# Moving half of the first layer's operand sums to GpSimd, and first-layer pieces two by two between the products

## The chip, the cores and the metric

The kernel runs on one core of a Trainium2 chip. The metric is the device time of one execution in microseconds (us), as the median of several runs. Engines are named as in the profile: PE is TensorE's matmuls and PEld its weight loads, DVE is VectorE, ACT is ScalarE, POOL is GpSimd, and SP is SyncE, which only issues DMAs here.

## What is computed

A small attention between tokens and states feeds a mixture of eight experts whose routing weights P come from a Sinkhorn iteration. Cut to what matters:

```python
# attention: x is (8, 8, 512, 64), state is (8, 8, 32, 64); their outputs side by side are 4352 rows of 512
logits = x @ w_gate                     # (N, 8), N = 4352
P = np.exp(logits - logits.max())
for _ in range(8):                      # Sinkhorn: rows, then columns
    P /= P.sum(1, keepdims=True) + 1e-09
    P /= P.sum(0, keepdims=True) + 1e-09
    P *= N / E
for e in range(8):
    h = np.maximum(x @ w1[e], 0.0)      # (N, 1024)
    ye = h @ w2[e]                      # (N, 512)
    out += P[:, e:e + 1] * ye
```

Every expert sees every row. The rows come in nine blocks: eight of 512 token rows, and one of 256 state rows.

## The kernel before

Up to about 142 us the kernel runs attention, routing and expert 0 in an order that a planner (`issue`, with costs and due times written into each `op`) lays out before launch. None of that part is touched. It ends with the first layer of (expert 1, block 0) and with Pmat, the routing weights.

Behind it lies the main part: `work` is a list of 63 units (experts 1 to 7, nine blocks each), and the order of each engine's instructions is the order in which the loop at the end of the kernel emits them. Each engine takes its instructions strictly in that order. Unit i runs the second layer of `work[i]` and, woven into it, the first layer of `work[i+1]` and the projection of `work[i+2]`.

**The second layer** (`layer2`) multiplies a 512 x 1024 hidden block by a 1024 x 512 matrix. It uses seven half-size products in place of eight (a Winograd scheme): the block and the matrix are cut in two by two, sums of the parts are multiplied, and the products are put together. In order, the seven products write the PSUM tiles A, E, Bseed, A, Bseed, E, Bseed (matmuls of line 271; PSUM is the accumulator memory that matmuls write). Each is eight matmuls of 256 columns, or four in block 8. After the first, ScalarE copies A into one of two Bseed tiles (line 305), on which later products pile up. After each of the other six, VectorE adds P times the product to `acc` in SBUF, one or two instructions of line 285 (in0 in PSUM, in1 in SBUF). A product that writes a tile again waits for the adds that read it.

**The operand sums.** The hidden tile is `Hm[128, 2, 4, 512]`: two halves of the hidden features (index i), four chunks of 128 (index j), and the tokens. The scheme needs sums of its quarters, s1, s2 and s4 in the tile `sm`, and a21 in place in `Hm`:

```python
nc.vector.tensor_add(s1, a21, a22)      # line 244
nc.vector.tensor_sub(a21, a11, a21)     # line 245
nc.vector.tensor_sub(s2, s1, a11)       # line 246
nc.vector.tensor_sub(s4, a12, s2)       # line 247
```

They are made in two halves of four instructions, for j = 0, 1 and for j = 2, 3, each 512 columns wide in float16 (256 for block 8). E, the second product, reads s1; the third (Bseed) reads s2; the fifth reads a21 and the sixth reads s4. Each of these takes its j = 0, 1 weights first.

**The first layer** (`layer1`) is a generator of eight pieces. A piece (0 to 7: j = 0 with i = 0, 1, then j = 1, and so on) makes 128 hidden features of a block: two matmuls of 512 columns (line 219), and a ReLU on ScalarE from PSUM to `Hm` (line 238). Its PSUM tiles come from a ring of four banks that the projection shares. The first half of the sums is emitted behind the fourth piece, and the second half behind the eighth. How many pieces follow each product stands in the loop as `(0, 0, 1, 2, 2, 2, 1)`; behind each `step()` a step of the weight loader can come.

**The projection** (`project`, lines 204 and 208) makes V, which the first layer of a token block reads: 16 narrow matmuls, put behind the first product, and four casts on ScalarE. Block 8 needs none, so the units of block 6 and the last two units have no projection.

**GpSimd** has three jobs in this part. `weigh` (line 254) multiplies the rows of `acc` by expert 0's weight, four instructions for each block (two for block 8), emitted in the units of expert 1: blocks 0 and 1 in the first unit, then block bi + 1 in unit bi. `load_w` issues the DMAs of the next expert's weights (lines 166 and 168) from block 1 on. They go through GpSimd's queue. And ten steps of the loop's count after that, with a step every sixth `step()`, VectorE makes the eight differences T of the second weight matrix (line 178); those left at the end of block 6 are emitted at once.

Of the kernel before, what the change touches and what calls it, by code (L numbers as in the profile page):

```python
# [12 lines left out]
ALU = mybir.AluOpType  # L13
AF = mybir.ActivationFunctionType
EPS = 1e-9


class Ring:
# [71 lines left out]
def kernel(  # L90
# [9 lines left out]
    nc = tc.nc  # L100
# [32 lines left out]
    def bank(shape, dtype, name, tag="bank"):  # L133
        return pools[tag].tile(shape, dtype, name=name, tag=tag)
# [25 lines left out]
    def load_w(e):  # L160

        w1h = mw.tile([128, NKC, F], FP16, name="w1h", tag="w1h")
        w2h = mw.tile([128, NFB, Dm], FP16, name="w2h", tag="w2h")
        w16[e] = (w1h, w2h)
        for g in range(2):
            nc.gpsimd.dma_start(out=w1h[:, ds(2 * g, 2), :], in_=w1r[e, :, ds(2 * g, 2), :])  # L166
        for g in range(2):
            nc.gpsimd.dma_start(out=w2h[:, ds(NJ * g, NJ), :], in_=w2r[e, :, ds(NJ * g, NJ), :])
        for _ in range(10):
            yield  # L170
        T = tpool[0].tile([128, 4, NJ, DH], FP16, name="T", tag="T")
        tsum[e] = T
        b11, b12 = w2h[:, :NJ, :DH], w2h[:, :NJ, DH:]
        b21, b22 = w2h[:, NJ:, :DH], w2h[:, NJ:, DH:]
        for i, (p, q) in enumerate(((b12, b11), (b22, T[:, 0]), (b22, b12), (b21, T[:, 1]))):
            for g in range(2):
                jj = ds(g * (NJ // 2), NJ // 2)
                nc.vector.tensor_sub(T[:, i, jj], p[:, jj], q[:, jj])
                yield
# [12 lines left out]
    def project(e, bi):  # L192
        if bi == B:
            return
        w1h = w16[e][0]
        V = vpool.tile([128, NQ, F], FP16, name="V", tag="V")
        vt[(e, bi)] = V
        for f in range(F // 512):
            cols = ds(f * 512, 512)
            ps = [bank([128, 512], FP32, "v_ps", ring[0]) for _ in range(NQ)]  # L200
            for j in range(4):
                for q in range(NQ):
                    r = ((j ^ q) % 2) * 64
                    nc.tensor.matmul(ps[q][ds(j * Ns, Ns), :], stT[ds(r, 64), bi, q, ds((j ^ q) * Ns, Ns)],  # L204
                                     w1h[ds(r, 64), 2 * q + j // 2, cols],
                                     tile_position=(r, j * Ns))
            for q in range(NQ):
                nc.scalar.copy(out=V[:, q, cols], in_=ps[q])  # L208

    def hidden_ps(e, bi, fb, out):  # L210
        w1h = w16[e][0]
        cols = ds(fb * 128, 128)
        if bi < B:
            V = vt[(e, bi)]
            terms = [(V[:, q, cols], aT[:, bi, q]) for q in range(NQ)]
        else:
            terms = [(w1h[:, kc, cols], xsT[:, kc]) for kc in range(NKC)]
        for k, (lhs, rhs) in enumerate(terms):
            nc.tensor.matmul(out, lhs, rhs, start=(k == 0), stop=(k == len(terms) - 1))  # L219
# [6 lines left out]
    def layer1(e, bi):  # L226

        t0, tn = blocks[bi]
        th = tn // 2
        Hm = hpool.tile([128, 2, NJ, S], FP16, name="Hm", tag="Hm")  # L230
        sm = hpool.tile([128, 3, NJ, S // 2], FP16, name="sm", tag="sm")
        hid[(e, bi)] = (Hm, sm)
        for j in range(NJ):
            for i in range(2):
                fb = i * NJ + j
                hps = bank([128, S], FP32, "hps", "h")
                hidden_ps(e, bi, fb, hps[:, :tn])
                nc.scalar.activation(out=Hm[:, i, j, :tn], in_=hps[:, :tn], func=AF.Relu)  # L238
                if j % 2 and i:
                    jj = ds(j - 1, 2)  # L240
                    a11, a21 = Hm[:, 0, jj, :th], Hm[:, 0, jj, th:tn]
                    a12, a22 = Hm[:, 1, jj, :th], Hm[:, 1, jj, th:tn]
                    s1, s2, s4 = (sm[:, k, jj, :th] for k in range(3))
                    nc.vector.tensor_add(s1, a21, a22)  # L244
                    nc.vector.tensor_sub(a21, a11, a21)  # L245
                    nc.vector.tensor_sub(s2, s1, a11)  # L246
                    nc.vector.tensor_sub(s4, a12, s2)  # L247
                yield

    def weigh(b):  # L250
# [92 lines left out]
    def op(rank, on, emit, after=(), takes=(), uses=(), also=()):  # L343
        o = Op(rank, on, emit, after, takes, uses, also)
        ops.append(o)
        return o
# [126 lines left out]
    for b in range(B):  # L473
# [23 lines left out]
        for q in range(NQ):  # L497
# [71 lines left out]
            s1 = op(r(4), {"DVE": (0.60, 0.80)}, subA, [m1], [], [eA, mxA])  # L569
# [71 lines left out]
    def tile_of(tag, shape):  # L641
        sm_[tag] = gsb.tile(shape, FP32, name=tag, tag=tag)
        return sm_[tag]
# [14 lines left out]
    for it in range(8):  # L658
        def rownorm():
            rsum = tile_of("rsum", [128, NTB])  # L660
            nc.vector.reduce_sum(out=rsum, in_=Pmat, axis=AX_X)
            nc.vector.tensor_scalar(out=rsum, in0=rsum, scalar1=EPS, scalar2=None, op0=ALU.add)
            nc.vector.reciprocal(out=rsum, in_=rsum)
# [5 lines left out]
        def colnorm(csb=csb):  # L669
            crec = tile_of("crec", [128, E])  # L670
            nc.vector.tensor_scalar(out=crec, in0=csb.tile, scalar1=EPS, scalar2=None, op0=ALU.add)
            nc.vector.reciprocal(out=crec, in_=crec)
# [176 lines left out]
    def step():  # L849
        nonlocal n  # L850
        n += 1
        if n % 6 == 0 and wload:
            try:
                next(wload[0])
            except StopIteration:
                wload.pop(0)

    work = [(e, bi) for e in range(1, E) for bi in range(len(blocks))]
    for i, (e, bi) in enumerate(work):
        if bi == 1 and e + 1 < E:  # L860
            wload.append(load_w(e + 1))
        l2 = layer2(e, bi, i)
        l1 = layer1(*work[i + 1]) if i + 1 < len(work) and work[i + 1] not in hid else iter(())
        for k in range(7):
            next(l2)
            step()
            if k == 0 and i + 2 < len(work) and work[i + 2] not in vt:
                project(*work[i + 2])
            for _ in range((0, 0, 1, 2, 2, 2, 1)[k]):
                next(l1, None)  # L870
                step()
        for part in (l1, l2):
            for _ in part:
                pass
        if bi == len(blocks) - 3:
            for _ in (x for w in wload for x in w):
                pass
            wload.clear()
# [30 lines left out]
```

## Time and profile before

| | |
|---|---|
| Time, three runs | 768.05 us median (767.78 to 769.49) |
| The profiled execution: time / span from first to last instruction | 766.84 us / 764.9 us |
| Granted TensorE clock over the span | 1.000 |
| Busy in an ordinary unit of 10.23 us (409.13 to 419.36) | PE 10.23, PEld 7.11, DVE 8.39, ACT 7.00, POOL 0.23 |
| Busy from 144 to 196 us (units of expert 1) | PE 52.00, PEld 35.52, DVE 45.09, ACT 35.47, POOL 51.99 |

A page of the profile lists each engine's busy time, then the span in 40 slices, the DMA queues, the chain of work that ended last, and groups of instructions. A row of a group reads: line, engine, operation, output<-inputs, shape, count | busy us in all, mean ns of one | idle us of the engine just before them, and who ended that idle time. A row of the chain reads: start, length, and what the chain went through. A row of a timeline reads: start, length, engine, line, operation. Matmul ends are modelled and overlap the next start, so the length of a product is best taken from start to start.

### The profile page before, as it was taken

The page shows a single profiled execution, that of the slowest core. Times are in us where ns is not written, and L with a number is a line of the kernel's source. Part 1 is how long each engine was busy: PE and PEld are TensorE (multiplying, and loading weights), DVE is VectorE, ACT ScalarE, POOL GpSimd, SP SyncE. Part 2 cuts the span into 40 slices and gives each one's busy share as a digit, 9 for nine tenths or more (in the row PEclk, how much of TensorE's full clock was granted, in tenths as well). Part 3 has the DMA queues.
Part 4 walks back from the last instruction along what each step waited for, and adds up shares of the span by engine and source line. Part 5 has one row for each costly group of instructions (what it writes and reads, how often), then busy time and mean ns, then how long its engine had stood idle before and what let it go on. Part 6 is the DMA issues. An engine that isn't in the chain of part 4 may idle for free.

```text
span 764.9 us, 16309 instructions
## 1 busy us (share of the span) xinstructions
PE 747.9 (98%) x6561; PEld 501.8 (66%) x6561; DVE 629.9 (82%) x1544; ACT 513.7 (67%) x1003; POOL 104.6 (14%) x102
## 2 busy tenths in 40 slices
PE   5999999999999999999999999999999999999997
PEld 3444445566776667766776767766677667766775
DVE  5998977888987888888887888888887888878886
ACT  5878976666667675766657666676657676576662
POOL 4433100799200000100001000100001000000000
PEclk9999999999999999999999999999999999999999
DMA  8997200060015000510006000240006000012234
GB/s 136 184 152 120 49 1 1 1 112 1 1 25 88 1 2 1 91 21 2 1 1 111 2 1 1 44 69 1 2 1 108 4 2 1 1 55 86 85 108 138
DMA packets 41595, 34.61 MB, mean 45 GB/s; under 512 B 16688, under 2 KB 33072, under 8 KB 41520
## 3 DMA queue, kind: packets, MB, share of 16 engines
q0 software_dynamic: 21248, 20.97, 17.7%
q1 hardware_dynamic: 19040, 12.08, 6.4%
q8 instruction: 51, 0.84, 0.4%
q10 hardware_dynamic: 1232, 0.52, 0.3%
q14 instruction: 24, 0.20, 0.1%
HBM read 42.48 MB, written 8.91 MB: 67 GB/s over the span
## 4 chain that ended last, share of the span: by engine, by line
PE 90%; DVE 5%; ACT 3%; DMA 1%; issue 0%; POOL 0%; POOLq 0%
PE hps L219 27%; PE Bseed L271 20%; PE E L271 14%; PE A L271 13%; PE yps L756 7%; PE v_ps L204 4%; PE hps L721 4%; DVE acc L285 2%; DMA x_nat<-in_x_dram 1%; DVE sm L244 1%; ACT V L357 1%; ACT Hm L238 1%; PE su_ps L596 1%; PE v_ps L699 0%; ACT xT L357 0%; PE ET_ps L581 0%
## 5 line engine op out<-in xcount | busy, mean ns | idle before, releaser
L238 ACT ACTIVATE Hm<-hps 128x512 f16<-128x512 f32 (+1 forms) x496 | 266.0, 572 | 188.5 <-PE hps L219 173.4
L219 PE MATMUL hps<-aT,V 128*128 128x512 f16 x880 | 234.8, 379 | 0.0
L271 PEld LDWEIGHTS <-Hm 128*128 128x128 f16 x1904 | 186.2, 98 | 69.8 <-issue 0.8
L285 DVE SCALAR_TENSOR_TENSOR acc<-Bseed,Pmat,acc 128x256 f32<-128x256 f32 x357 | 156.9, 479 | 56.9 <-PE Bseed L271 54.4
L271 PEld LDWEIGHTS <-sm 128*128 128x128 f16 x1428 | 134.2, 98 | 52.5 <-DVE sm L244 24.2
L271 PE MATMUL Bseed<-T,Hm 128*128 128x256 f16 x952 | 124.5, 273 | 0.4 <-DVE acc L285 0.3
L271 PE MATMUL A<-w2h,Hm 128*128 128x256 f16 x952 | 124.7, 273 | 0.0
L219 PEld LDWEIGHTS <-V 128*128 128x128 f16 x880 | 86.1, 98 | 45.2
L208 ACT CAST V<-v_ps 128x512 f16<-128x512 f32 x216 | 111.3, 610 | 0.0
L285 DVE SCALAR_TENSOR_TENSOR acc<-E,Pmat,acc 128x256 f32<-128x256 f32 x238 | 104.3, 477 | 3.7
L244 DVE TENSOR_TENSOR sm<-Hm 128x512 f16<-128x512 f16 (+1 forms) x124 | 51.7, 417 | 19.1 <-ACT Hm L238 18.3
L756 PE MATMUL yps<-w2h,hT 128*128 128x512 f16 x272 | 66.5, 380 | 0.0
L285 DVE SCALAR_TENSOR_TENSOR acc<-A,Pmat,acc 128x256 f32<-128x256 f32 x119 | 52.4, 479 | 15.8 <-PE A L271 15.7
L271 PE MATMUL E<-T,sm 128*128 128x256 f16 x476 | 64.5, 274 | 0.7
L271 PE MATMUL Bseed<-T,sm 128*128 128x256 f16 x476 | 62.4, 273 | 0.0
L271 PE MATMUL E<-w2h,sm 128*128 128x256 f16 x476 | 62.3, 273 | 0.0
L254 POOL TENSOR_SCALAR acc<-acc,Pmat 128x512 f32<-128x512 f32 x34 | 55.2, 1638 | 44.8 <-DVE Pmat L673 44.8
L166 POOL DMA_DIRECT2D w1h<-in_moe_w_dram x12 | 8.6, 721 | 355.2 <-PE hps L219 355.2
L247 DVE TENSOR_TENSOR sm<-Hm,sm 128x512 f16<-128x512 f16 (+1 forms) x124 | 53.1, 428 | 4.2
L245 DVE TENSOR_TENSOR Hm<-Hm 128x512 f16<-128x512 f16 (+1 forms) x124 | 51.6, 416 | 4.3
L246 DVE TENSOR_TENSOR sm<-sm,Hm 128x512 f16<-128x512 f16 (+1 forms) x124 | 50.0, 403 | 0.0
L305 ACT COPY Bseed<-A 128x512 f32<-128x512 f32 (+1 forms) x63 | 34.4, 546 | 18.8 <-PE A L271 17.3
(107 smaller groups left out, 554.1 us busy)
## 6 DMA issues: line engine op xcount, KB each, us to landing
w1h<-in_moe_w_dram POOLq DMA_DIRECT2D x16, 512.0 KB, 7.2
w2h<-in_moe_w_dram POOLq DMA_DIRECT2D x16, 512.0 KB, 7.5
out_dram<-acc SPq DMA_DIRECT2D x32, 256.0 KB, 2.8
x_nat<-in_x_dram POOLq DMA_DIRECT2D x16, 256.0 KB, 6.3
st_st<-in_state_dram SPq DMA_DIRECT2D x1, 256.0 KB, 4.2
st_st<-in_state_dram ACTq DMA_DIRECT2D x1, 256.0 KB, 4.6
out_dram<-acc SPq DMA_DIRECT2D x4, 64.0 KB, 1.9
out_dram<-acc ACTq DMA_DIRECT2D x4, 64.0 KB, 2.1
```

Source lines behind the costliest of these rows:

```text
L208: nc.scalar.copy(out=V[:, q, cols], in_=ps[q])
L219: nc.tensor.matmul(out, lhs, rhs, start=(k == 0), stop=(k == len(terms) - 1))
L238: nc.scalar.activation(out=Hm[:, i, j, :tn], in_=hps[:, :tn], func=AF.Relu)
L244: nc.vector.tensor_add(s1, a21, a22)
L245: nc.vector.tensor_sub(a21, a11, a21)
L246: nc.vector.tensor_sub(s2, s1, a11)
L247: nc.vector.tensor_sub(s4, a12, s2)
L254: nc.gpsimd.tensor_scalar(out=acc[:, k, :], in0=acc[:, k, :], scalar1=Pmat[:, k, 0:1], scalar2=None, op0=ALU.mult)
L271: nc.tensor.matmul(dst[:, c], lhs(j, c), rhs[:, j], start=first and c == 0 and j == 0, stop=(j == NJ - 1), skip_group_check=True)
L285: nc.vector.scalar_tensor_tensor(out=dst, in0=src[:, c], scalar=p[:, k], in1=dst, op0=ALU.mult, op1=ALU.add)
L305: nc.scalar.copy(out=Bb[:, :nk], in_=A[:, :nk])
L756: nc.tensor.matmul(yps.tile, hT[fb].tile[:, ds(tk * 128, 128)], w2h[:, fb, :], start=(fb == 0), stop=(fb == NFB - 1))
```

## The change

The four sums of the first half (j = 1) are issued on GpSimd and not on VectorE; those of the second half (j = 3) stay on VectorE. This holds for the 62 first layers that the loop makes, and not for the one in the planner's part. The pattern of pieces changes from one, two, two, two and one behind products 3 to 7 to two behind each of products 3 to 6, and none behind the seventh. So the second half of the sums stands in VectorE's queue ahead of the seventh product's adds, where it stood behind them.

```diff
+PAT = (0, 0, 2, 2, 2, 2, 0)
...
-                    nc.vector.tensor_add(s1, a21, a22)
-                    nc.vector.tensor_sub(a21, a11, a21)
-                    nc.vector.tensor_sub(s2, s1, a11)
-                    nc.vector.tensor_sub(s4, a12, s2)
+                    (nc.vector if j > 1 else nc.gpsimd).tensor_add(s1, a21, a22)
+                    (nc.vector if j > 1 else nc.gpsimd).tensor_sub(a21, a11, a21)
+                    (nc.vector if j > 1 else nc.gpsimd).tensor_sub(s2, s1, a11)
+                    (nc.vector if j > 1 else nc.gpsimd).tensor_sub(s4, a12, s2)
...
-            for _ in range((0, 0, 1, 2, 2, 2, 1)[k]):
+            for _ in range(PAT[k]):
```

All lines behind the new one stand one number higher in the changed kernel: its sums are lines 245 to 248. In the built program GpSimd's queue runs, behind the planner's part: 8 weighings, 4 sums, 4 weighings, 4 weight DMAs, 4 sums, 4 weighings, 4 sums, and so on by fours to 2 weighings and 4 sums; then four sums for each unit, with four DMAs once for each expert. ScalarE's and SyncE's orders are the same as before.

## The prediction

> **What bounds the kernel now.** I read the page first: its busy shares and the chain that ended last.
>
> ```profile
> PE 747.9 (98%) x6561; PEld 501.8 (66%) x6561; DVE 629.9 (82%) x1544; ACT 513.7 (67%) x1003; POOL 104.6 (14%) x102
> ...
> PE 90%; DVE 5%; ACT 3%; DMA 1%; issue 0%; POOL 0%; POOLq 0%
> ```
>
> TensorE is never idle for long and GpSimd nearly always. So I next read the chain in order of time, for two stretches behind 144 us, where the 63 units (7 experts x 9 blocks) run:
>
> ```profile
> 194.49 0.87 PE A L271 x8
> 195.36 0.56 PE v_ps L204 x16
> 195.92 1.01 PE E L271 x8
> 196.93 0.87 PE Bseed L271 x8
> 197.80 0.43 PE hps L219 x2
> ...
> 203.62 0.34 DVE T L178
> 203.96 1.57 DVE acc L285 x4
> 205.53 0.34 DVE sm L244
> 205.87 0.05 issue
> 205.91 0.83 PE E L271 x6
> ```
>
> A product takes 0.87 us, a first-layer piece 0.43, a projection 0.56; the chain passes from one to the next without a gap. By matmul starts an ordinary unit is 10.23 us (409.13 to 419.36). The only loss is where E waits for the second-half sums: in the second stretch, a unit without a projection (block 6), E takes 1.12 us from its first matmul to the next product's. There are eight such units, each losing 0.22 to 0.25, and all products together lose some 2.7 us behind 144 us. That is all that relief of VectorE can bring: 0.35%.
>
> **What moves.** 62 first layers have two halves of four sums each. The first half, 248 operations, leaves VectorE, where one of 512 columns takes 0.42 (103 us in all), for GpSimd. The groups by shape price it:
>
> ```profile
> L244 DVE TENSOR_TENSOR sm<-Hm 128x512 f16<-128x512 f16 x110 | 47.6, 433 | 19.1 <-ACT Hm L238 18.3
> L254 POOL TENSOR_SCALAR acc<-acc,Pmat 128x512 f32<-128x512 f32 x34 | 55.2, 1638 | 44.8 <-DVE Pmat L673 44.8
> L559 POOL TENSOR_TENSOR a<-eA,rA 128x512 f16<-128x512 f32 x12 | 12.5, 1045 | 52.6 <-DVE rA L556 20.9 <-DVE nsB L535 12.9 <-ACT V L357 5.8
> L539 DVE TENSOR_TENSOR eA<-eA,mxA 128x512 f32<-128x512 f32 x16 | 11.4, 710 | 0.1
> ```
>
> No GpSimd operation with two float16 inputs is in the trace. Nearest is L559: two inputs, 512 columns, 1.045. Farther off are the weighing (one input, 1.64) and a 128-column memset (0.20, so 0.8 for four). I take 1.045; the ends are 0.8 and 1.64. The built program makes the second and fourth sum wait for the one before on GpSimd; a wait costs about 0.1 (Pmat ends at 138.00, the weighing starts at 138.11). Four sums: 4 x 1.045 + 0.2 = 4.4 us. The Trainium skill (GPSIMD Engine Reference, section 3.1) gives 4497 ns for an add of 2048 float32 columns, a quarter of which is 1.12, an estimate; the sum below would be 4 us larger by it.
>
> **The two engines get in each other's way.** The timeline shows it twice:
>
> ```profile
> 84.14 1.04 POOL L559 TENSOR_TENSOR a<-eA,rA 128x512 f16<-128x512 f32 x1 [12.90 <-DVE nsB L535]
> ...
> 84.61 1.13 DVE L539 TENSOR_TENSOR eA<-eA,mxA 128x512 f32<-128x512 f32 x1
> ```
>
> ```profile
> 150.69 0.88 DVE L244 TENSOR_TENSOR sm<-Hm 128x512 f16<-128x512 f16 x1 [0.18 <-ACT Hm L238]
> 151.61 0.43 DVE L245 TENSOR_TENSOR Hm<-Hm 128x512 f16<-128x512 f16 x1
> ```
>
> L539 needs 0.69 alone; started inside a GpSimd operation it ended 0.54 after that one's end, so it got its data only then. A float16 sum should end some 0.28 after the GpSimd operation it meets. Under the weighing a sum takes 0.42 or up to 0.98, and a weighing that a sum got into 1.93 to 2.00 in place of 1.55. L285, with one operand in PSUM, stays at 0.47: the adds are free of it. The Trainium skill (SBUF — State Buffer, "Who interferes with whom") says that a VectorE instruction with two SBUF inputs and a GpSimd one that reads SBUF exclude each other, whole instructions. The two-input pair agrees; the weighing does not, since sums of 0.42 run wholly inside one. By the rule alone, sums in (a) would wait out weighings of up to 1.55; the trace excludes it, so it has no chance of its own.
>
> **An ordinary unit, in us from its first A.** New order: A 0, projection 0.97, E 1.53, Bseed 2.41, two pieces 3.28, A 4.15, two pieces 5.02, Bseed 5.88, two 6.75, E 7.62, two 8.49, Bseed 9.36, end 10.23. A ReLU starts 0.65 after its piece, lasts 0.60, the second of a pair starts 0.49 later: the fourth ends at 6.76, the eighth at 10.23. GpSimd: s1 to 7.9, a21 to 9.05, s2 to 10.1, s4 to 11.25. VectorE's half meets only that last one: its s1 ends at 11.5, a21 11.95, s2 12.35, s4 12.8. The next unit's E reaches the second half at 11.98 and its Bseed at 12.86, their weights some 0.2 earlier. No stall, with 0.25 to spare; before, the spare was much the same. So earlier pieces and relief of VectorE are spent on the slower half. The pairs cost nothing: four PSUM banks, and the ReLU two pieces back has ended before its bank is asked for again. The adds of Bseed end 0.9 before the product that overwrites it.
>
> **Where it stalls.**
> (a) First expert. GpSimd now runs in order 8 weighings, sums, 4 weighings, 4 weight DMAs, sums, 4 weighings, sums. Today it runs ahead of the sums:
>
> ```profile
> 149.07 8.17 POOL L254 TENSOR_SCALAR acc<-acc,Pmat 128x512 f32<-128x512 f32 x5
> 157.19 1.50 POOL L166 DMA_DIRECT2D w1h<-in_moe_w_dram  x2
> 158.69 1.52 POOL L168 DMA_DIRECT2D w2h<-in_moe_w_dram  x2
> ```
>
> Eight weighings end at 150.6, sums 155.1, four weighings (6.2) 161.3, DMAs (3.0) 164.3. Then s1 is ready at 165.45 and s2 at 167.65, while unit 2 (from 163.6) wants them near 165.1 and 166.4: a stall of 1.6. From there GpSimd's period is 6.2 + 4.4 + 0.1 = 10.7 against 10.23: 0.6 in unit 3, 0.5 in units 4, 5 and 7, 1.05 in unit 6, none in unit 8 behind a half weighing. Sum 4.8, with 0.7 for sums that get into weighings: 5.5.
> (b) The unit of block 8 has products of half length, 7.13 us in all (402.00 to 409.13), but makes a full first layer. The fourth ReLU ends 2.1 before the next A, s2 on GpSimd at 410.35, s4 behind VectorE's s1 at 411.65; VectorE's s2 is ready at 412.4, Bseed wants it at 411.6: 0.8, six times, 4.8.
> (c) At the end of block 6 four T differences (0.34 each by starts) stand behind the sums in VectorE's queue, which now end at 12.8, or 2.57 of the next unit. Two adds (0.40 each by starts), the four, E's two adds and Bseed's two follow: 2.57 + 0.8 + 1.36 + 0.8 + 0.8 = 6.33. The product at 5.88 that overwrites Bseed waits some 0.5; six experts: 3.0. Before, those adds ended 0.4 ahead of it (219.50 and 219.87).
> (d) Block 6: the 0.25 at E becomes some 0.33, eight times: 0.7.
> The weight DMAs of later experts stand behind sums in GpSimd's queue and are issued some 18 us later (402.43 to about 421), but T, their first reader, comes four units after: nothing. If that cover were gone, T would hold VectorE's adds.
> Sum 5.5 + 4.8 + 3.0 + 0.7 = 14.0. The profiled execution was 766.84 around a span of 764.9, so it becomes 780.8; the median shown lies 1.2 above it: 782.
>
> **Rivals.**
> Quick sums (faster or same): at 0.8 a sum, GpSimd's four end at 10.26, as the eighth ReLU does. Then (b) and (c) vanish, (a) shrinks to 1.2, and block 6's loss, 2.0, is won: about 767. Without the DMAs' stall too, 765.5. For it: float16 halves the bytes; VectorE's 0.42 against 0.69 shows that its engine gains by that. Against it: L559's output is float16 already. It decides where four sums take under 3.4 us.
> Slow sums: from 1.2 a sum the ordinary units stall as well. At 1.2: 0.1 in some 36 of them, (a) 8.5, (b) 6.6, (c) 4.5: 792. At 1.3: 0.5 each, (a) 11.5, (b) 9, (c) 6: about 813. At 1.64, above 850.
> Pairs stall TensorE: if a ReLU of a pair ran so late that a bank was missing, each pair would lose up to 0.49. ScalarE is 68% busy in a unit, which speaks against; 785 to 800 if it is one pair a unit.
>
> **How the numbers follow.** Forecast (GpSimd's queue and the exclusion, 772 to 795) 0.72; slow sums 0.10; pairs 0.02; quick sums 0.16, of which half gain over 0.2% (1.5 us, about what a measurement of this kernel can tell). That gives faster 0.08, same 0.08, slower 0.84. The range runs from 768, quick sums without a gain, to 800, between slow sums of 1.2 and 1.3.
>
> **What would show it.** After: GpSimd rows of L245 to L248 near 1045 ns and some 250 us busy; VectorE 95 to 100 us less; TensorE gaps at E and Bseed in units 2 to 7 of the first expert and behind each block 8, with "POOL sm" and "DVE sm" as releasers; none in ordinary units. VectorE's remaining sums longer than 0.42 for the first of four. Wrong if the GpSimd rows are under 0.85 us, or if TensorE waits in units of blocks 1 to 5.

## The result, and the profile after

The changed kernel takes 787.17 us (median of 4 runs, 785.86 to 788.65) against 767.92 (767.78 to 769.49): slower by a ratio of 1.0252 (95% interval 1.0235 to 1.0268). The forecast was 782, with a range of 768 to 800.

Three lines of the page: engines and busy time and the chain by engine, which the prediction shows of before, and the chain by line.

```profile
PE 751.8 (96%) x6561; PEld 499.5 (64%) x6561; DVE 595.4 (76%) x1296; ACT 507.5 (65%) x1003; POOL 382.7 (49%) x350
...
POOL 40%; issue 36%; PE 16%; DVE 3%; DMA 2%; ACT 2%; POOLq 0%; DVEq 0%
POOL sm L248 9%; POOL Hm L246 9%; POOL sm L245 8%; POOL sm L247 8%; PE yps L757 7%; POOL acc L255 4%; PE hps L722 4%; POOL w2h L169 1%; PE hps L220 1%; DMA x_nat<-in_x_dram 1%; PE Bseed L272 1%; DMA xT<-x_nat 1%; POOL w1h L167 1%; DVE Hm L246 1%; PE A L272 1%
```

GpSimd has gone from 14% to 49% of the span, and TensorE's matmuls from 98% to 96%. The chain needs care: it follows the engine that was last released, so it now runs through GpSimd in all units. But most units lose nothing. Where time is lost is seen by measuring each unit from the start of its first A matmul to that of the next one:

| Unit | before, us | after, us |
|---|---|---|
| Expert 1, blocks 0 and 1 | 10.91, 10.31 | 10.91, 10.34 |
| Expert 1, blocks 2, 3, 4, 5 | 10.23, 10.23, 10.23, 10.26 | 12.73, 11.54, 11.33, 11.33 |
| Expert 1, blocks 6, 7 | 9.82, 10.27 | 11.72, 13.27 |
| Later experts, block 0 | 10.23 | 11.00 (six times) |
| Later experts, blocks 1 to 5 | 10.23 | 10.23 |
| Experts 2 to 6, block 6 | 9.82 | 10.20 or 9.80 |
| Experts 2 to 6, block 7 | 10.27 to 10.29 | 10.68 to 10.71 |
| Expert 7, blocks 6, 7 | 9.80, 9.84 | 9.80, 9.85 |
| All experts, block 8 | 7.17 | 7.17 |

From the first unit on the kernel is 18.8 us longer: 10.9 in expert 1, 4.7 in the block 0 units, 2.1 in block 7 and 1.1 in block 6, and nothing in the last unit (the expectations below say 18.6, which is slightly short). The profiled execution (788.42) also took 2.8 us longer before the first unit, which the change doesn't touch; with the runs spread over 2.8 us, the comparisons below go by units.

The groups by shape price the moved sums and what is left on VectorE:

```profile
L248 POOL TENSOR_TENSOR sm<-Hm,sm 128x512 f16<-128x512 f16 x55 | 71.8, 1305 | 4.3
L246 DVE TENSOR_TENSOR Hm<-Hm 128x512 f16<-128x512 f16 x55 | 64.3, 1168 | 1.9
L247 POOL TENSOR_TENSOR sm<-sm,Hm 128x512 f16<-128x512 f16 x55 | 64.2, 1168 | 0.0
L246 POOL TENSOR_TENSOR Hm<-Hm 128x512 f16<-128x512 f16 x55 | 64.1, 1165 | 4.3
L245 POOL TENSOR_TENSOR sm<-Hm 128x512 f16<-128x512 f16 x55 | 63.5, 1154 | 243.9 <-ACT Hm L239 243.9
L245 DVE TENSOR_TENSOR sm<-Hm 128x512 f16<-128x512 f16 x55 | 35.6, 648 | 38.2 <-POOL sm L247 23.7 <-ACT Hm L239 14.5
```

An undisturbed GpSimd sum takes 1.15 us. On VectorE the mean of L245 is 0.65 and that of L246 1.17, where 0.42 was usual. The timelines show why. First an ordinary unit of expert 2, GpSimd's and then VectorE's:

```profile
263.37 1.15 POOL L245 TENSOR_TENSOR sm<-Hm 128x512 f16<-128x512 f16 x1 [2.35 <-ACT Hm L239]
264.60 1.15 POOL L246 TENSOR_TENSOR Hm<-Hm 128x512 f16<-128x512 f16 x1
265.72 1.15 POOL L247 TENSOR_TENSOR sm<-sm,Hm 128x512 f16<-128x512 f16 x1
266.94 1.35 POOL L248 TENSOR_TENSOR sm<-Hm,sm 128x512 f16<-128x512 f16 x1
```

```profile
266.86 0.42 DVE L245 TENSOR_TENSOR sm<-Hm 128x512 f16<-128x512 f16 x1 [0.74 <-POOL sm L247]
267.32 1.26 DVE L246 TENSOR_TENSOR Hm<-Hm 128x512 f16<-128x512 f16 x1
268.50 0.41 DVE L247 TENSOR_TENSOR sm<-sm,Hm 128x512 f16<-128x512 f16 x1
268.95 0.42 DVE L248 TENSOR_TENSOR sm<-Hm,sm 128x512 f16<-128x512 f16 x1
```

VectorE's s1 slips in ahead of GpSimd's s4, which becomes 0.2 longer. Its a21 then waits s4 out and ends 0.28 after it (268.58 and 268.30). The two engines meet once, and TensorE has just enough slack. In expert 1 the four weighings ahead of the sums hold them back, until they start only just before VectorE's half (GpSimd, then VectorE):

```profile
189.99 1.15 POOL L245 TENSOR_TENSOR sm<-Hm 128x512 f16<-128x512 f16 x1
191.22 1.22 POOL L246 TENSOR_TENSOR Hm<-Hm 128x512 f16<-128x512 f16 x1
192.40 1.33 POOL L247 TENSOR_TENSOR sm<-sm,Hm 128x512 f16<-128x512 f16 x1
193.81 1.21 POOL L248 TENSOR_TENSOR sm<-Hm,sm 128x512 f16<-128x512 f16 x1
195.00 6.35 POOL L255 TENSOR_SCALAR acc<-acc,Pmat 128x512 f32<-128x512 f32 x4
201.32 1.15 POOL L245 TENSOR_TENSOR sm<-Hm 128x512 f16<-128x512 f16 x1
```

```profile
190.74 0.69 DVE L245 TENSOR_TENSOR sm<-Hm 128x512 f16<-128x512 f16 x1 [0.67 <-ACT Hm L239]
191.46 1.26 DVE L246 TENSOR_TENSOR Hm<-Hm 128x512 f16<-128x512 f16 x1
192.64 1.37 DVE L247 TENSOR_TENSOR sm<-sm,Hm 128x512 f16<-128x512 f16 x1
194.05 1.26 DVE L248 TENSOR_TENSOR sm<-Hm,sm 128x512 f16<-128x512 f16 x1
```

GpSimd has no idle time: its period, 189.99 to 201.32, is 11.33 us, which is the length of units 4 and 5. And now every sum of VectorE waits for one of GpSimd: four take 4.6 us in place of 1.7.

What TensorE itself waits for is read from a list of waits: who waited, for whom, and the us in all, the times and the longest. The first two lines are of the unit of expert 1 just shown (190.7 to 202.1 us), the others of blocks 0, 6 and 7 of expert 2 (from 245.5, 307.6 and 317.8 us):

```profile
PE Bseed L272 <- POOL sm L247: 0.5, 1, 0.5
PE Bseed L272 <- DVE acc L286: 0.2, 1, 0.2
PE Bseed L272 <- DVE sm L247: 0.6, 1, 0.6
PE E L272 <- DVE sm L245: 0.5, 1, 0.5
PE Bseed L272 <- DVE acc L286: 0.3, 1, 0.3
```

In that unit of expert 1 TensorE waits for GpSimd's s2, and later for adds that VectorE makes behind its held sums. In expert 2 it waits for VectorE alone: for its s2 in block 0, its s1 in block 6, and its adds in block 7.

### The profile page after: what moved, and what is told of

Same layout as the page of the kernel before. It is cut to its first block, busy times and chain, and to the rows that moved or that the text cites. A ratio compares the mean times of both kernels' runs of the same rounds, so it can differ in the third digit from the quotient of the medians.

```text
span 786.5 us, 16547 instructions
## 1 busy us (share of the span) xinstructions
PE 751.8 (96%) x6561; PEld 499.5 (64%) x6561; DVE 595.4 (76%) x1296; ACT 507.5 (65%) x1003; POOL 382.7 (49%) x350
## 4 chain that ended last, share of the span: by engine, by line
POOL 40%; issue 36%; PE 16%; DVE 3%; DMA 2%; ACT 2%; POOLq 0%; DVEq 0%
POOL sm L248 9%; POOL Hm L246 9%; POOL sm L245 8%; POOL sm L247 8%; PE yps L757 7%; POOL acc L255 4%; PE hps L722 4%; POOL w2h L169 1%; PE hps L220 1%; DMA x_nat<-in_x_dram 1%; PE Bseed L272 1%; DMA xT<-x_nat 1%; POOL w1h L167 1%; DVE Hm L246 1%; PE A L272 1%
## 5 line engine op out<-in xcount | busy, mean ns | idle before, releaser
L239 ACT ACTIVATE Hm<-hps 128x512 f16<-128x512 f32 (+1 forms) x496 | 259.7, 573 | 165.2 <-PE hps L220 162.0
L220 PE MATMUL hps<-aT,V 128*128 128x512 f16 x880 | 225.8, 379 | 0.0
L245 POOL TENSOR_TENSOR sm<-Hm 128x512 f16<-128x512 f16 (+1 forms) x62 | 68.1, 1099 | 275.1 <-ACT Hm L239 275.1
L272 PEld LDWEIGHTS <-sm 128*128 128x128 f16 x1428 | 132.5, 98 | 68.0 <-POOL sm L248 14.6
L248 POOL TENSOR_TENSOR sm<-Hm,sm 128x512 f16<-128x512 f16 (+1 forms) x62 | 76.4, 1233 | 4.9
L272 PE MATMUL Bseed<-T,sm 128*128 128x256 f16 x476 | 64.7, 273 | 9.4 <-DVE sm L247 4.7
L246 POOL TENSOR_TENSOR Hm<-Hm 128x512 f16<-128x512 f16 (+1 forms) x62 | 68.8, 1109 | 4.9
L245 DVE TENSOR_TENSOR sm<-Hm 128x512 f16<-128x512 f16 (+1 forms) x62 | 37.7, 608 | 41.5 <-POOL sm L247 23.7
L247 POOL TENSOR_TENSOR sm<-sm,Hm 128x512 f16<-128x512 f16 (+1 forms) x62 | 68.9, 1111 | 0.0
L246 DVE TENSOR_TENSOR Hm<-Hm 128x512 f16<-128x512 f16 (+1 forms) x62 | 66.3, 1069 | 2.1
```

The source lines that it names most:

```text
L245: (nc.vector if j > 1 else nc.gpsimd).tensor_add(s1, a21, a22)
L246: (nc.vector if j > 1 else nc.gpsimd).tensor_sub(a21, a11, a21)
L247: (nc.vector if j > 1 else nc.gpsimd).tensor_sub(s2, s1, a11)
L248: (nc.vector if j > 1 else nc.gpsimd).tensor_sub(s4, a12, s2)
L272: nc.tensor.matmul(dst[:, c], lhs(j, c), rhs[:, j], start=first and c == 0 and j == 0, stop=(j == NJ - 1), skip_group_check=True)
```

## The experiments

Three theories stood against each other. **Queue**: in expert 1, weighings and sums together overfill GpSimd. **Meeting**: sums on the two engines exclude each other, so VectorE's half comes late wherever GpSimd's isn't done before it. **Pattern**: the pairs of pieces, or sums ahead of adds, cost something by themselves. The kernel before ran beside each set of four, at 767.39 us both times (17 and 23 runs).

**The pattern alone**

```diff
-(nc.vector if j > 1 else nc.gpsimd)     # four times, in the changed kernel
+nc.vector
```

> The new pattern of pieces, with all sums on VectorE. If the loss comes from GpSimd (its queue and its meeting with VectorE's sums), nothing of the 18.6 us that the main part lost is left: the second half of the sums stands 0.87 us earlier, the 0.22 to 0.25 us at E in the eight units without a projection go, and the time is 766 to 768. If the pairs of pieces cost TensorE something (the rival), ordinary units are longer than 10.23 us and the time is over 771.

769.60 us (12 runs), ratio 1.0030 (1.0017 to 1.0042): a small loss, neither of the two answers. Ordinary units are 10.23, so pairs cost nothing, and block 6 comes down to 9.57, the 0.25 that were hoped for. But every block 8 goes from 7.17 to 7.62, and blocks 0 to 4 of expert 1 lose 0.2 to 0.5 each. The timelines of a block 8 unit, VectorE's and then TensorE's, show the cost:

```profile
230.16 0.43 DVE L245 TENSOR_TENSOR sm<-Hm 128x512 f16<-128x512 f16 x1 [1.10 <-ACT Hm L239]
230.62 0.42 DVE L246 TENSOR_TENSOR Hm<-Hm 128x512 f16<-128x512 f16 x1
230.96 0.42 DVE L247 TENSOR_TENSOR sm<-sm,Hm 128x512 f16<-128x512 f16 x1
231.41 0.42 DVE L248 TENSOR_TENSOR sm<-Hm,sm 128x512 f16<-128x512 f16 x1
231.75 0.48 DVE L286 SCALAR_TENSOR_TENSOR acc<-Bseed,Pmat,acc 128x256 f32<-128x256 f32 x1
```

```profile
232.29 0.60 PE L272 MATMUL Bseed<-T,Hm 128*128 128x256 f16 x4 [0.29 <-DVE acc L286]
```

The first half's sums, which wait for a late ReLU, now stand ahead of the fifth product's add, and the last product waits for that add. In blocks 0 to 4 of expert 1 it is the same product that waits: there weighings run beside these sums (one takes 0.80 at 181.21). With the first half on GpSimd block 8 is back at 7.17, and blocks 0 and 1 of expert 1 go from 11.13 and 10.78 to 10.91 and 10.34: the places where the move helps TensorE.

**GpSimd alone, with the old pattern**

```diff
-PAT = (0, 0, 2, 2, 2, 2, 0)
+PAT = (0, 0, 1, 2, 2, 2, 1)
```

> The first half of the sums on GpSimd, with the old pattern. The fourth piece's ReLU then ends 0.8 us later and the eighth's too. If the meeting of the two engines' sums sets the loss, GpSimd's s2 ends at 11.2 of a unit, VectorE's s1 at 11.5, its a21 behind GpSimd's s4 at 12.9, its s2 at 13.3, and Bseed, which wants it at 12.65, waits 0.7 in each of some 36 ordinary units: 810 to 820. If only GpSimd's full queue in expert 1 counts, the ordinary units stay at 10.23 and the time is within 3 us of the changed kernel's 787.

808.73 us, ratio 1.0536 (1.0514 to 1.0558). Blocks 1 to 5 of later experts go from 10.23 to 10.62, and block 0 to 11.35. So the ordinary units do lose without the earlier pieces, as the meeting has it, by 0.40 each and not 0.7: as in the changed kernel, VectorE's s1 gets in ahead of GpSimd's s4, and only its a21 is held (1.26, as a group mean). The two parts of the change belong together: of the 41 us that GpSimd's sums cost with the old pattern, the new one takes off 22.

**Expert 1's sums back on VectorE**

```diff
-(nc.vector if j > 1 else nc.gpsimd)
+(nc.vector if j > 1 or e == 1 else nc.gpsimd)
```

> The changed kernel, but with expert 1's sums on VectorE, where GpSimd still has the weighings. If GpSimd's queue in expert 1 is the cause of 10.9 of the 18.6 us, they go and the rest stays: 776, with units 2 to 7 of expert 1 at 10.23 (9.6 without the projection) and the 0.78 and 0.4 us behind and ahead of each later block 8 as before. If the loss of expert 1 came from something else in those units, it stays: 785 or more.

776.19 us, ratio 1.0115 (1.0097 to 1.0133), as expected. Units 2 to 5 of expert 1 (blocks 2 to 5) come down to 10.45, 10.53, 10.53 and 10.23 and not all to the expected 10.23 (the pattern alone has the same), unit 6 to 9.57, unit 7 to 10.27; all later units stay as in the changed kernel.

**Weighings of half the columns**

```diff
-nc.gpsimd.tensor_scalar(out=acc[:, k, :], in0=acc[:, k, :], ...
+nc.gpsimd.tensor_scalar(out=acc[:, k, :DH], in0=acc[:, k, :DH], ...
```

> The changed kernel with weighings of 256 columns in place of 512: the second half of each row of acc is left unweighed. GpSimd's period in expert 1 falls from 11.33 us by some 3 us to about 8.3, under the unit's 10.23. If the length of GpSimd's queue sets the loss there, units 3 to 5 come back to 10.23, unit 2 keeps at most 1 us for the four weight DMAs, and 8 to 10 us go: 777 to 779. If the sums' meeting with VectorE's alone set it, whatever else GpSimd has to do, units 3 to 5 stay near 11.3 and the time near 787.

776.69 us, ratio 1.0123 (1.0102 to 1.0143). The second half of each row is left unweighed. All sums of the first half are still on GpSimd, and units 3 to 5 are back at 10.23. Unit 2, where the four DMAs stand ahead of the sums, keeps 0.93, and unit 7 keeps 0.73. GpSimd's timeline has idle time again:

```profile
185.61 4.04 POOL L255 TENSOR_SCALAR acc<-acc,Pmat 128x256 f32<-128x256 f32 x4
190.99 1.16 POOL L245 TENSOR_TENSOR sm<-Hm 128x512 f16<-128x512 f16 x1 [1.34 <-ACT Hm L239]
```

So most of expert 1's loss goes when GpSimd's queue is shorter. Where GpSimd gets done in time, meeting once costs nothing there either.

**Block 0's sums on VectorE**

```diff
-(nc.vector if j > 1 else nc.gpsimd)
+(nc.vector if j > 1 or bi == 0 else nc.gpsimd)
```

> The changed kernel, but with the sums of each block 0 (made beside block 8's short products) on VectorE. If GpSimd's late s4 and its meeting with VectorE's sums in that short unit cost the 0.78 us at each block 0, those go, six times, 4.7 us; VectorE's first-half sums then stand ahead of the adds in the short unit, which cost 0.45 there with the pattern alone, so 0.45 x 6 = 2.7 come back: 785, with block 0 at 10.23 and block 8 at 7.62. If the 0.78 belongs to the pairs of pieces in the short unit, block 0 stays at 11.0 and the time at 787 or above.

786.61 us, ratio 1.0251 (1.0234 to 1.0267). Block 0 is back at 10.23 and block 8 at 7.62 to 7.69, so both mechanisms are confirmed, with 0.07 more in block 8 than expected. They nearly cancel: from the first unit on it is 1.5 us shorter than the changed kernel by units, which the medians (786.61, 787.17) hardly show.

**GpSimd only in blocks 1 to 5 of experts 2 to 7**

```diff
-(nc.vector if j > 1 else nc.gpsimd)
+(nc.gpsimd if j == 1 and e > 1 and 1 <= bi <= 5 else nc.vector)
```

> The changed kernel with GpSimd's sums in blocks 1 to 5 of experts 2 to 7 alone: 30 first layers, 120 operations, 50 us of VectorE's time. In all other units the sums are on VectorE. If relief of VectorE is worth nothing where TensorE is the limit, each of these units stays at 10.23 us and the time is that of the pattern alone, 769 to 770.5. If relief is worth something that the stalls elsewhere hid, units get shorter than 10.23 and the time falls below 768. If GpSimd's sums cost even there, it is above 772.

769.03 us, ratio 1.0021 (1.0009 to 1.0032): that of the pattern alone. Every one of the thirty units it touches stays at 10.23. Relief of VectorE is worth nothing there, and GpSimd's sums cost nothing.

**GpSimd's half earlier, VectorE's in place**

```diff
-PAT = (0, 0, 2, 2, 2, 2, 0)
+PAT = (0, 2, 2, 1, 1, 2, 0)
```

> The changed kernel with pieces two behind the second product, two behind the third, one each behind the fourth and fifth, two behind the sixth. The eighth piece stands where it stood; the fourth, and so GpSimd's sums, come 1.7 us earlier. If the meeting of the two engines' sums causes what is lost outside expert 1, GpSimd is done before VectorE starts: VectorE's sums fall back to 0.42 us, the 0.78 at block 0, the 0.4 in block 7 and the 0.4 in block 6 go, together some 8 us, and expert 1, where GpSimd's queue has no slack, keeps most of its 10.9: 778 to 781. If it is the later place of VectorE's sums ahead of the adds, or the pairs, the 8 us stay: 786 to 789.

773.96 us, ratio 1.0086 (1.0070 to 1.0102): more came back than expected. In later experts block 0 is at 10.23, block 7 at 10.27, block 6 at 9.57, and block 8 at 7.33 (0.16 more). The sums hardly meet, in an ordinary unit of expert 2 (GpSimd's last of one unit, then VectorE's):

```profile
259.52 1.15 POOL L248 TENSOR_TENSOR sm<-Hm,sm 128x512 f16<-128x512 f16 x1
```

```profile
260.32 0.64 DVE L245 TENSOR_TENSOR sm<-Hm 128x512 f16<-128x512 f16 x1 [0.74 <-ACT Hm L239]
260.99 0.42 DVE L246 TENSOR_TENSOR Hm<-Hm 128x512 f16<-128x512 f16 x1
261.33 0.42 DVE L247 TENSOR_TENSOR sm<-sm,Hm 128x512 f16<-128x512 f16 x1
261.79 0.43 DVE L248 TENSOR_TENSOR sm<-Hm,sm 128x512 f16<-128x512 f16 x1
```

Only VectorE's s1 still meets the end of GpSimd's s4 and is held for 0.2. The loss outside expert 1 is gone. This run alone can't tell a late GpSimd from a held VectorE, since it makes GpSimd's half early too; but the waits that the changed kernel's list shows in expert 2 were for VectorE, so the loss there was the meeting's.

Units 2 to 7 of expert 1 still lose 7.7 us (0.87 to 0.94 in units 3 to 5, a period near 11.1 to 11.2). GpSimd's queue runs late there all the same, and the sums still meet one by one (VectorE in unit 4):

```profile
187.39 1.37 DVE L246 TENSOR_TENSOR Hm<-Hm 128x512 f16<-128x512 f16 x1
188.68 1.37 DVE L247 TENSOR_TENSOR sm<-sm,Hm 128x512 f16<-128x512 f16 x1
190.09 1.26 DVE L248 TENSOR_TENSOR sm<-Hm,sm 128x512 f16<-128x512 f16 x1
```

So this run doesn't part queue and lock-step in expert 1, and why some 3 of the 10.9 came back isn't shown. The expectation had left out that gain, and block 6's.

**The pattern where it pays**

The kernel before, all sums on VectorE, with the new pattern only in the eight units that make the sums for a unit without a projection:

```diff
+            new = bi == 5 or (e == E - 1 and bi == 6)
-            for _ in range((0, 0, 1, 2, 2, 2, 1)[k]):
+            for _ in range(((0, 0, 2, 2, 2, 2, 0) if new else (0, 0, 1, 2, 2, 2, 1))[k]):
```

> The kernel before, with the new pattern in the units of block 5 alone, and of block 6 in the last expert; all sums on VectorE. These eight units make the sums for a unit without a projection. If the 0.22 to 0.25 us at E there is all that the change can win, eight such are won, 2.0 us, with nothing lost: 765.4 where the kernel before has 767.4, ratio 0.9974. If the pattern costs as much elsewhere in these units, the ratio is 1.000.

765.68 us (12 runs) against 767.39 (23 runs): ratio 0.9972 (0.9961 to 0.9983), the only version here faster than the kernel before. The eight units get shorter by 0.23 to 0.25 each, and no unit gets longer. Its chain passes block 6 of expert 1 without the stop that the prediction showed:

```profile
204.37 0.87 PE A L271 x8
205.25 0.87 PE E L271 x8
206.12 0.87 PE Bseed L271 x8
```

## Why the prediction was right, point by point

- **What bounds the kernel** held. No run gained more than the bound of 2.7 us: by units 2.0 of it was for the taking (1.7 by the medians), by the pattern alone in eight units, without GpSimd.
- **Ordinary units** held exactly: 10.23 before and after, in spite of 248 operations moved. Removing the early pieces (808.73) showed that the slack had been real and small.
- **Price of a GpSimd sum**: 1.045 was taken from L559; the rows say 1.15. The Trainium skill's figure (GPSIMD Engine Reference, section 3.1), a quarter of which is 1.12, an estimate for float32, was nearer: the trace agrees with it within 3%. The nearest row has a broadcast operand and float32 inputs; which of these makes its 0.1 wasn't tried.
- **Exclusion** held: a VectorE sum ends 0.28 after the GpSimd sum that it meets. In an ordinary unit it is the second of VectorE's four that is held, not the first, which slips in; in block 0 the first is held as well (1.26 at 246.00).
- **(a) first expert**: the place and the mechanism were right, the size was not: 5.5 (6.0 with its share of (c)) against 10.9. This term is nearly the whole gap between 14.0 and 18.8. GpSimd's period was set at 10.7 and measured 11.33: the weighings took 6.3, near the 6.2 that were set, but the four sums 5.0, not 4.4, by 0.4 for their own length and the rest for meeting. The price explains only a part: the prediction's own two cases (5.5 at 1.045 and 8.5 at 1.2) put the term near 7.5 at 1.15, an estimate. What the sum also lacked is that late GpSimd sums meet all four of VectorE's, so that VectorE is late too. That shows most in unit 7, which lost 3.0 and was forecast at 1.0 with (c): there TensorE waits 1.2 for VectorE's s2 and 1.2 for adds, with T differences queued as well. How the rest divides between queue and meeting no run shows. That the full queue starts it two runs show: all but 1.2 of the 10.9 goes with the sums (776.19), and all but 1.4 with half of each weighing (776.69).
- **(b) block 0**: 0.8 forecast, 0.78 measured, six times; it goes when GpSimd's half is early, and when these sums are back on VectorE.
- **(c) T differences**: 0.5 forecast, 0.42 measured in block 7 of experts 2 to 6.
- **(d) block 6**: 0.7 forecast, 1.1 measured, 0.38 in three experts and none in the others, so that the sum came near was in part luck. In experts 2, 4 and 6 a T difference (1.11 at 306.95) stands just ahead of VectorE's s1, which then meets GpSimd's s4 and is held (1.37 at 307.99); E loses 0.64 where it lost 0.25. In experts 3, 5 and 7 s1 slips in, a21 is held, and Bseed loses 0.24 in E's place.
- **The weight DMAs** issued later cost nothing in experts 2 to 6, as forecast.
- **Rivals.** Quick sums fell with the 1.15. Slow sums begin at 1.2, and 1.15 was below it (1.20 is the mean of the four rows with the held sums in it, and ordinary units still didn't stall). The pairs cost nothing in ordinary units, but the pattern itself had a cost that no rival named: sums ahead of adds, 0.45 in block 8 where they are on VectorE.
- **VectorE's busy time** was to fall by 95 to 100 us and fell by 34.5: the remaining sums, and some T differences, wait inside their own rows for GpSimd.

## What to carry to other kernels

Work that is moved to an idle engine is worth what the bounding engine was waiting for and no more: here 2.7 us of waits at most, against 103 us of VectorE's time moved. Price the move by the unit in which the receiving engine is already full, and not by its average (14% over the span, 100% in expert 1), and lay out both engines' operations on one time axis, since two that exclude each other are late together. And where a schedule helps in some units and hurts in others, use it only where it helps.

## What the runs showed of the hardware

GpSimd's weighing, with one float32 input, takes longer than its float16 sum with two: 1.55 us for 512 columns undisturbed and 1.01 for 256, against 1.15 and 0.67 for sums. Where both engines had a run of dependent sums at the same time, in expert 1 of the changed kernel, they went in lock-step: three of VectorE's four went from 0.42 to between 1.26 and 1.37, and GpSimd's from 1.15 to as much as 1.33.
